# Hashed attention beside a gated feed-forward layer: a unit's maximum is spread three steps behind its own transposes

## The chip, the cores and the metric

The kernel runs on one core of a Trainium2 chip. The metric is the device time of one execution in microseconds; three executions of the kernel as it stood are given below, and one more was recorded by the hardware profiler. The engines are TensorE (PE in the rows, with its weight loads as PEld), VectorE (DVE), ScalarE (ACT), GpSimd (POOL) and SyncE (SP), which issues most transfers.

## The reference

```python
# attention: 2 batches, 8 heads, 768 positions, 64 columns a head
q_bucket = np.sum(((q @ proj) > 0) * 2 ** np.arange(6), axis=-1)   # k_bucket likewise
mask = q_bucket[:, :, :, None] == k_bucket[:, :, None, :]
scores = np.where(mask, scale * np.matmul(q, k.transpose(0, 1, 3, 2)), -1e9)
scores = scores - np.max(scores, axis=-1, keepdims=True)
attn = np.exp(scores); attn = attn / (attn.sum(-1, keepdims=True) + 1e-9)
x = np.matmul(attn, v)                       # then reshaped to 1536 x 512
# layer 1: w_gate, w_val 512 x 1536, w_out 1536 x 512
g = x @ w_gate
x = (g / (1 + np.exp(-g)) * (x @ w_val)) @ w_out
# layer 2: w_in 512 x 2048, w_out 2048 x 512
h = x @ w_in
out = (np.maximum(h, 0) + alpha * np.minimum(h, 0)) @ w_out
```

## The kernel before

**The attention** is cut into 24 items (a batch, a pair of heads, 256 queries), and each item into two units, one for each head: 48 units. A unit passes through four parts, each a Python generator whose yields are the steps that the rest of the kernel counts:

- `banks` (three steps): the scores S of 768 keys by 256 queries, two 128-key blocks to a PSUM bank (L283, L284, tag S, three banks); ACT copies each bank to the SBUF tile `se` (L285); DVE takes maxima over the blocks into `m2`, of which there is one buffer (L291, L293).
- `top` (one step, `s_mt`): PE transposes `m2` (tile `mt`, L303, and L309 in the second chunk, behind a DVE maximum on L307), and DVE reduces it to the maximum of each query, `mq` (L304 or L310).
- `back` (one step): `s_mb` transposes `mq` again, spread over all partitions (tile `mb`, L315); `s_sub` subtracts it from the scores on DVE (L320, 128 x 1536); `s_exp` takes the exponential on ACT (L325).
- `values` (three steps): six pairs of matmuls `po` with the values (L333), and behind the second head the denominators and the rounding of the result (L339 to L362).

The four parts of different units are woven together. A list gives each part a slot: that of the unit's number plus 0, 1, 2 and 3 (`LAGS`, L33). From slot 6 on a slot holds, in this order, the `banks` of unit s, the `top` of unit s-1, the `back` of unit s-2 and the `values` of unit s-3: eight steps. So a unit's `back` comes nine steps behind its `top`, and its `values` nine steps behind its `back`.

**The layers.** Tokens go through in three chunks of 512. The attention of chunk 0 (16 units) runs with the preparation of the first weights alone; the bank tag of `mt` and `mb` is then G, with two banks. From there on `stage1(0)` and `stage1(1)`, layer 1 of chunks 0 and 1, run with the attention of chunks 1 and 2 beside them: the main loop takes 1.9 attention steps for each yield of `stage1` (`RATES`). In this part of the program `mt` and `mb` both lie in the tag T (L812), and T has one bank (L779):

```python
    at.nb = dict(S=3, T=1, G=2, Y=1, po=1)
    at.tag = dict(m="T", hp="S", po=("po", "po"))
```

`stage1(2)` and the three `stage2` calls then run without attention. Layer matmuls are L642 to L644 (tiles `gp` and, in layer 2, `hp`) and L647 to L649 (`op`), each 128 x 512; the gates' work on DVE is L622 and L625, on ACT L619 and L634, on POOL L637. In `stage1(0)` each weight is read from memory for the first time as raw 64-bit words and converted: L539 on ACT, L540 and L542 on DVE, L544 on POOL, then split into two parts on ACT (L579) and on POOL or DVE in turn (L586).

The order of the work on each engine follows the order of these calls, except that the framework's scheduler lets an instruction whose inputs and buffers are free pass one that has to wait. Each engine executes its own list in order.

Of the kernel before, what the change touches and what calls it, by code (L numbers as in the profile page):

```python
# [32 lines left out]
LAGS = (0, 1, 2, 3)  # L33

OLDER = 6
# [13 lines left out]
def lsh_attention_moe_kernel(  # L49
# [19 lines left out]
    GQ = 256  # L69
    NG = S // GQ  # L70
    NPAIR = H // 2
# [4 lines left out]
    W = 512  # L76
# [74 lines left out]
    def load_v(it):  # L151

        t = at.sm.tile([P, NC, 3 * D], F32, tag="vv", name="vv", bufs=4)
        VV[it.b, it.p] = t
        nc.gpsimd.memset(t[:, :, D:2 * D], 1.0)
        for x in range(2):
            nc.sync.dma_start(out=t[:, :, 2 * x * D:(2 * x + 1) * D], in_=vP[it.b, 2 * it.p + x])

    def load_k(it):

        it.nat = wp.tile([P, S], F32, tag="raw64", name="nat", bufs=RAWB)
        nc.sync.dma_start(out=it.nat, in_=kview2(it))
        nc.gpsimd.dma_start(out=KA(it)[0:D], in_=kview(it))

    def load_q(it, eng=nc.sync):
        it.qr = at.sm.tile([P, 2, GQ], F32, tag="qr", name="qr", bufs=2)
        eng.dma_start(out=it.qr, in_=qview(it))
# [56 lines left out]
    def prep(it):  # L224

        def rest():
            pass

        todo = []
        if it.first:  # L230
            todo += [lambda x=x: rest_k(it, x, nc.gpsimd if POOL_K[x] else nc.vector) for x in range(2)]
            todo += [lambda x=x: copy_k(it, x) for x in range(2)]
        if it.first and it.b > 0:
            todo += [lambda: load_v(it)]
        todo += [lambda: round_q(it), lambda: rest_q(it)] + [rest] * (1 if it.first else 4)
        if it.first:
            todo += hash_k(it, 0) + hash_k(it, 1)
        todo += hash_q(it)
        last = todo[-1]

        def end():
            last()
            it.ready = True

        todo[-1] = end
        return todo

    def load(it):
        if it.first and it.b > 0:
            load_k(it)  # L250
        load_q(it)
# [7 lines left out]
    def first_item(it):  # L259
        ka, kb = KA(it), KB(it)  # L260
        for x in range(2):
            nc.scalar.activation(out=ka[0:D, x], in_=it.nat[x * D:(x + 1) * D, :], func=AF.Copy)
        round_q(it)
        for x in range(2):
            rest_k(it, x, nc.vector)
        nc.vector.tensor_tensor(out=it.QB[0:D], in0=it.qr[0:D], in1=f32(it.QA)[0:D], op=ALU.subtract)
        for x in range(2):
            nc.scalar.activation(out=kb[0:D, x], in_=it.nat[x * D:(x + 1) * D, :], func=AF.Copy)
        for fn in hash_q(it) + hash_k(it, 0, "G") + hash_k(it, 1, "G"):
            fn()  # L270
        it.ready = True

    def s_bank(u, j):
        it = u.it
        if j == 0:
            u.se = at.sm.tile([P, NC, GQ], F32, tag="se", name="se", bufs=at.nse)
        pt = at.ps.tile([P, 2, GQ], F32, tag="S", name="S", bufs=at.nb["S"])
        u.pt.append(pt)
        qa, qb = it.QA[:, u.x, :], it.QB[0:KR, u.x, :]
        ka, kb = KA(it)[:, u.x, :], KB(it)[0:KR, u.x, :]  # L280
        for i in range(2):
            sl = slice((2 * j + i) * P, (2 * j + i + 1) * P)
            nc.tensor.matmul(pt[:, i, :], lhsT=ka[:, sl], rhs=qa, start=True, stop=False)  # L283
            nc.tensor.matmul(pt[:, i, :], lhsT=kb[:, sl], rhs=qb, start=False, stop=True)  # L284
        nc.scalar.activation(out=u.se[:, 2 * j:2 * j + 2, :], in_=pt, func=AF.Copy)  # L285

    def s_max(u, j):

        if j == 1:
            u.m2 = at.sm.tile([P, 2, GQ], F32, tag="m2", name="m2", bufs=1)  # L290
            nc.vector.tensor_tensor(out=u.m2, in0=u.pt[1], in1=u.se[:, 0:2, :], op=ALU.max)  # L291
        else:
            nc.vector.scalar_tensor_tensor(out=u.m2, in0=u.pt[2], scalar=FLOOR, in1=u.m2, op0=ALU.max, op1=ALU.max)  # L293
            u.pt = None

    def s_mt(u):

        tp = at.ps.tile([P, 2, 2, P], F32, tag=at.tag["m"], name="mt", bufs=at.nb[at.tag["m"]])
        u.mq = at.sm.tile([P, 2, 1], F32, tag="mq", name="mq", bufs=2)
        if at.halves:  # L300
            for j in range(2):
                for h in range(2):
                    nc.tensor.transpose(tp[:, j, h, :], u.m2[:, h, j * P:(j + 1) * P], ident)  # L303
            nc.vector.tensor_reduce(out=u.mq, in_=tp.rearrange("p a b c -> p a (b c)"), axis=AX.X, op=ALU.max)  # L304
        else:
            m1 = u.m2[:, 0, :]
            nc.vector.tensor_tensor(out=m1, in0=m1, in1=u.m2[:, 1, :], op=ALU.max)  # L307
            for j in range(2):
                nc.tensor.transpose(tp[:, j, 0, :], m1[:, j * P:(j + 1) * P], ident)  # L309
            nc.vector.tensor_reduce(out=u.mq, in_=tp[:, :, 0, :], axis=AX.X, op=ALU.max)  # L310

    def s_mb(u):
        bc = at.ps.tile([P, 2, P], F32, tag=at.tag["m"], name="mb", bufs=at.nb[at.tag["m"]])
        for j in range(2):
            nc.tensor.transpose(bc[:, j, :], u.mq[:, j, :].to_broadcast([P, P]), ident)  # L315
        u.mx = bc.rearrange("p a b -> p (a b)")

    def s_sub(u):

        nc.vector.scalar_tensor_tensor(  # L320
            out=u.se, in0=u.se, scalar=FLOOR, in1=u.mx[:, None, :].to_broadcast([P, NC, GQ]),
            op0=ALU.max, op1=ALU.subtract)

    def s_exp(u):
        nc.scalar.activation(out=u.se, in_=u.se, func=AF.Exp, scale=SCALE)  # L325
# [31 lines left out]
    def s_xh(it):  # L357
        nc.scalar.activation(out=xcols(it)[0], in_=it.xf, func=AF.Copy)
# [7 lines left out]
    for b in range(B):  # L366
        order = [(p, g) for g in range(NG) for p in range(NPAIR)]
# [10 lines left out]
    def attention():  # L378

        us = []  # L380
        for it in items:
            for x in range(2):
                u = Bag()
                u.it, u.x, u.pt = it, x, []
                us.append(u)
        todo = []

        def queue(i):

            if i + 2 < len(items):  # L390
                todo.extend(prep(items[i + 2]))
            if i + 3 < len(items):
                n = 2 if items[i + 2].first and i > 0 else 1
                todo.insert(min(len(todo), n), lambda: load(items[i + 3]))

        def step():

            for _ in range(2 if at.alone else 1):
                if todo:
                    todo.pop(0)()  # L400

        load_k(items[1])
        load_q(items[1])
        load_v(items[0])
        first_item(items[0])
        for i in (2, 3):
            load_k(items[i])
            load_v(items[i - 1])
        load_q(items[2])
        load_v(items[3])  # L410
        todo.extend(prep(items[1]))

        def banks(u):
            for j in range(3):
                s_bank(u, j)
                if j == 2:
                    s_max(u, 1)
                step()
                yield
            s_max(u, 2)  # L420
            if u.x == 1:
                queue(u.it.i)

        def top(u):
            s_mt(u)
            step()
            yield

        def back(u):
            s_mb(u)  # L430
            s_sub(u)
            s_exp(u)
            step()
            yield

        def values(u):
            for j in range(3):
                s_pv(u, j)
                if j == 2 and u.x == 1:
                    s_den(u.it)  # L440
                    s_out(u.it)
                    s_xh(u.it)
                    s_xl(u.it)
                step()
                yield

        order = []
        for i, u in enumerate(us):
            for k, part in enumerate((banks, top, back, values)):
                slot = i + LAGS[k]  # L450
                order.append(((slot, i, k) if slot < OLDER else (slot, k, i), part, u))
        order.sort(key=lambda o: o[0])
        for _, part, u in order:
            if part is banks:
                while not u.it.ready:
                    todo.pop(0)()
            yield from part(u)
# [33 lines left out]
    late = [w for w in o2 if w not in early]  # L491
# [290 lines left out]
    first_load(items[0])  # L782
    setup()
    side = attention()

    def more():
# [17 lines left out]
    k = 0  # L804
# [103 lines left out]
```

## Time and profile before

| | |
|---|---|
| median of three executions | 874.92 us (872.17 to 876.06) |
| the profiled execution, its own time | 873.3 us |
| its span, first to last instruction | 871.5 us |
| PE busy | 824.7 us, 95% |
| DVE busy | 525.4 us, 60% |
| ACT busy | 448.4 us, 51% |
| POOL busy | 364.5 us, 42% |

The stretches of the span: attention of chunk 0 alone to about 128 us; layer 1 of chunk 0 with the attention of chunk 1 beside it to about 305 us and a little beyond; layer 1 of chunk 1 with the last attention to about 480 us; layer 1 of chunk 2 to about 605 us; layer 2 to the end. A busy share says how much of a stretch an engine had an instruction in work; matmuls overlap in the pipeline, so PE's idle time is read from what the rows print in brackets (the idle time before an instruction, and what ended it).

### The profile page before, as it was taken

What the parts mean: (1) busy time and instruction counts of PE and PEld (TensorE: products, weight loads), DVE (VectorE), ACT (ScalarE), POOL (GpSimd) and SP (SyncE); (2) the same over time, 40 slices, a digit from 0 to 9 for tenths busy, and PEclk for the clock granted to TensorE, in tenths of its full rate; (3) what the DMA queues carried; (4) which work ended last, traced back from release to release, by engine and by line L of the source; (5) the groups of instructions that cost most, each with busy time, mean ns of one, the idle gap of its engine ahead of it and who ended that gap; (6) DMA issues with size and microseconds to landing.
All of it is one profiled execution on the core that took longest, in us unless ns stands there. A gap on an engine that the chain in (4) does not pass through costs nothing.

```text
span 871.5 us, 11218 instructions
## 1 busy us (share of the span) xinstructions
PE 824.7 (95%) x4022; PEld 685.0 (79%) x4022; DVE 525.4 (60%) x789; ACT 448.4 (51%) x738; POOL 364.5 (42%) x304
## 2 busy tenths in 40 slices
PE   5989889899989999999999998989999999999997
PEld 3777777687777888888888786877888888888886
DVE  5877979888878856666665373645433343334332
ACT  6877977687766654655543233313333333334331
POOL 4211527675554533322322353623544354435441
PEclk9999999999999999999999999999999999999999
DMA  9120356786565437555445678886000300010001
GB/s 218 57 73 25 111 163 203 226 279 226 184 227 184 158 133 265 170 181 180 157 159 193 213 257 291 313 283 223 1 0 1 146 1 1 0 49 1 1 0 49
DMA packets 57287, 122.03 MB, mean 140 GB/s; under 512 B 16912, under 2 KB 29200, under 8 KB 56720
## 3 DMA queue, kind: packets, MB, share of 16 engines
q1 hardware_dynamic: 56080, 118.51, 39.9%
q0 software_dynamic: 1008, 2.75, 1.6%
q8 instruction: 32, 0.52, 0.2%
q14 instruction: 23, 0.19, 0.1%
q10 hardware_dynamic: 144, 0.05, 0.0%
HBM read 94.03 MB, written 27.26 MB: 139 GB/s over the span
## 4 chain that ended last, share of the span: by engine, by line
PE 62%; DVE 12%; DMA 10%; ACT 9%; issue 4%; POOL 2%; SPq 0%; ACTq 0%; DVEq 0%; POOLq 0%
PE po L333 8%; DMA raw<-in_wblk_dram 7%; PE gp L643 6%; PE gp L642 6%; PE gp L644 6%; PE op L648 5%; PE hp L643 5%; PE hp L644 5%; PE op L647 5%; PE op L649 5%; PE hp L642 5%; DMA wb<-w 2%; PE S L283 2%; PE S L284 2%; ACT se L285 2%
## 5 line engine op out<-in xcount | busy, mean ns | idle before, releaser
L637 POOL TENSOR_TENSOR gl<-ex,gh 128x512 fp32r<-128x512 f32 x84 | 110.2, 1311 | 183.5 <-ACT gh L634 183.3
L333 PE MATMUL po<-se,vv 128*128 128x256 f32 x576 | 143.6, 384 | 3.7 <-ACT se L325 3.7
L642 PE MATMUL gp<-xh,wb 128*128 128x512 f32 x288 | 121.2, 421 | 4.0 <-DMA wb<-w 3.9
L333 PEld LDWEIGHTS po<-se,vv 128*128 128x128 f32 x576 | 106.5, 191 | 20.4 <-ACT se L325 5.2
L628 DVE TENSOR_SCALAR ex<-hp,al 128x512 f32<-128x512 f32 x48 | 36.1, 751 | 135.7 <-PE hp L644 135.7
L644 PE MATMUL gp<-xh,wb 128*128 128x512 f32 x288 | 113.1, 393 | 0.0
L643 PE MATMUL gp<-xl,wb 128*128 128x512 f32 x288 | 112.9, 392 | 0.0
L634 ACT ACTIVATE gh<-ex 128x512 fp32r<-128x512 f32 x84 | 52.9, 630 | 107.1 <-DVE ex L631 67.8
L579 ACT ACTIVATE wb<-w 128x512 fp32r<-128x512 f32 x96 | 60.4, 631 | 92.1 <-PE hp L644 78.2
L544 POOL TENSOR_TENSOR wt<-wt,wr 128x512 int32<-128x512 int32 x48 | 63.5, 1327 | 87.3 <-DVE wt L542 44.7
L325 ACT ACTIVATE se<-se 128x1536 f32<-128x1536 f32 x48 | 71.3, 1485 | 49.7 <-DVE se L320 49.5
L285 ACT ACTIVATE se<-S 128x512 f32<-128x512 f32 x144 | 80.2, 592 | 22.9 <-PE S L284 19.1
L320 DVE SCALAR_TENSOR_TENSOR se<-se,mb 128x1536 f32<-128x1536 f32 x48 | 83.8, 1746 | 3.2 <-PE mb L315 3.1
L283 PE MATMUL S<-QA,kt 128*128 128x256 f32 x288 | 81.7, 310 | 2.8 <-ACT se L285 1.6
L284 PE MATMUL S<-qb,kt 76*128 76x256 f32 x288 | 75.4, 291 | 2.7 <-ACT qb L204 1.7
L642 PE MATMUL hp<-xh,wb 128*128 128x512 f32 x192 | 74.7, 389 | 0.0
L643 PE MATMUL hp<-xl,wb 128*128 128x512 f32 x192 | 74.7, 389 | 0.0
L644 PE MATMUL hp<-xh,wb 128*128 128x512 f32 x192 | 74.7, 389 | 0.0
L647 PE MATMUL op<-wb,gh 128*128 128x512 f32 x192 | 74.7, 389 | 0.0
L648 PE MATMUL op<-wb,gh 128*128 128x512 f32 x192 | 74.7, 389 | 0.0
L649 PE MATMUL op<-wb,gl 128*128 128x512 f32 x192 | 74.7, 389 | 0.0
L586 POOL TENSOR_TENSOR wb<-w,wb 128x512 fp32r<-128x512 f32 x48 | 62.3, 1297 | 23.7 <-ACT wb L579 23.7
(98 smaller groups left out, 1667.8 us busy)
## 6 DMA issues: line engine op xcount, KB each, us to landing
wb<-w SPq DMA_DIRECT2D x72, 512.0 KB, 4.0
raw<-in_wblk_dram SPq DMA_DIRECT2D x68, 512.0 KB, 4.3
w<-wb SPq DMA_DIRECT2D x36, 512.0 KB, 3.1
qr<-in_q_dram SPq DMA_DIRECT2D x24, 256.0 KB, 3.0
nat<-in_k_dram SPq DMA_DIRECT2D x8, 384.0 KB, 3.6
vv<-in_v_dram SPq DMA_DIRECT2D x16, 192.0 KB, 5.2
whole<-wt SPq DMA_DIRECT2D x12, 256.0 KB, 2.1
w<-whole SPq DMA_DIRECT2D x12, 256.0 KB, 6.3
```

The costliest lines, as they stand in the source:

```text
L283: nc.tensor.matmul(pt[:, i, :], lhsT=ka[:, sl], rhs=qa, start=True, stop=False)
L284: nc.tensor.matmul(pt[:, i, :], lhsT=kb[:, sl], rhs=qb, start=False, stop=True)
L285: nc.scalar.activation(out=u.se[:, 2 * j:2 * j + 2, :], in_=pt, func=AF.Copy)
L320: nc.vector.scalar_tensor_tensor(out=u.se, in0=u.se, scalar=FLOOR, in1=u.mx[:, None, :].to_broadcast([P, NC, GQ]), op0=ALU.max, op1=ALU.su ...
L333: nc.tensor.matmul(it.po[:, u.x, :], lhsT=VV[it.b, it.p][:, kb, u.x * D:u.x * D + P], rhs=u.se[:, kb, :], start=kb == 0, stop=kb == NC - 1)
L637: nc.gpsimd.tensor_tensor(out=l, in0=ex, in1=f32(h), op=ALU.subtract)
L642: nc.tensor.matmul(pt, lhsT=h, rhs=ah, start=first, stop=False)
L643: nc.tensor.matmul(pt, lhsT=h, rhs=al_, start=False, stop=False)
L644: nc.tensor.matmul(pt, lhsT=l, rhs=ah, start=False, stop=last)
L647: nc.tensor.matmul(pt, lhsT=gh, rhs=h, start=first, stop=False)
L648: nc.tensor.matmul(pt, lhsT=gh, rhs=l, start=False, stop=False)
L649: nc.tensor.matmul(pt, lhsT=gl, rhs=h, start=False, stop=last)
```

## The change

From unit 14 on (2 x 4 x 2 - 2), `back` gets the slot of the unit's number plus 1, and stands last in it. A slot from 16 on then holds the `banks` of unit s, the `top` of unit s-1, the `values` of unit s-3 and the `back` of unit s-1. A unit's `back` comes four steps behind its own `top`, with the three steps of an older unit's `values` in between, and its `values` come thirteen steps behind its `back`. Nothing is added or removed.

```diff
         order = []
         for i, u in enumerate(us):
+            beside = i >= 2 * NPAIR * (W // GQ) - 2
             for k, part in enumerate((banks, top, back, values)):
-                slot = i + LAGS[k]
-                order.append(((slot, i, k) if slot < OLDER else (slot, k, i), part, u))
+                slot = i + (1 if part is back and beside else LAGS[k])
+                late = 4 if part is back and beside else k
+                order.append(((slot, i, k) if slot < OLDER else (slot, late, i), part, u))
         order.sort(key=lambda o: o[0])
```

In the changed program every line below these has a number higher by two: L642 becomes L644, L540 becomes L542, L542 becomes L544, L586 becomes L588.

**PE, one unit beside layer 1 of chunk 0** (the transposes that the trace of before has at 170.11 us). Here `mt` and `mb` are the two users of the bank T, `gp` is layer 1, `hp` the hashes, `po` the values. Before:

```order
L303 MATMUL mt<-ident,m_1572 128x128 x4
L642 MATMUL gp<-xh,wb 128x512
L643 MATMUL gp<-xl,wb 128x512
L644 MATMUL gp<-xh,wb 128x512
L642 MATMUL gp<-xh,wb 128x512
L643 MATMUL gp<-xl,wb 128x512
L644 MATMUL gp<-xh,wb 128x512
L192 MATMUL hp<-kt_124,skh 44x384
L315 MATMUL mb<-ident,mq 128x128 x2
L193 MATMUL hp<-kt_124,skl 44x384
```

Of the change, the same unit; the first piece left out is three more `hp` and six `gp`, the second the rest of six `gp`:

```order
L303 MATMUL mt<-ident,m_1577 128x128 x4
L333 MATMUL po<-se,vv 128x256 x2
L192 MATMUL hp<-kt_124,skh 44x384
...
L333 MATMUL po<-se,vv 128x256 x4
L644 MATMUL gp<-xh,wb 128x512
...
L315 MATMUL mb<-ident,mq 128x128 x2
L192 MATMUL hp<-kt_124,skh 44x384
```

Between the four `mt` and the two `mb` stood six `gp` and one `hp`; now there are twelve `gp`, six `po` and four `hp`. From `mb` to the next four `mt` there were eighteen `gp`, twelve `S`, six `po` and ten `hp`; now there are twelve `gp`, twelve `S` and eight `hp`, four of them of 256 columns.

**DVE, the same unit.** Before, from the first maximum of the next unit to the subtraction L320:

```order
L291 TENSOR_TENSOR m_1572<-S,se 128x512
L304 TENSOR_REDUCE mq<-mt 128x2
L293 SCALAR_TENSOR_TENSOR m_1572<-S,m_1572 128x512
L625 SCALAR_TENSOR_TENSOR ex<-ex,gp 128x512
L320 SCALAR_TENSOR_TENSOR se<-se,mb 128x1536
L542 SCALAR_TENSOR_TENSOR wt<-raw_1620,wt 128x512
L586 TENSOR_TENSOR wb<-wt,wb 128x512
```

Of the change:

```order
L291 TENSOR_TENSOR m_1577<-S,se 128x512
L304 TENSOR_REDUCE mq<-mt 128x2
L293 SCALAR_TENSOR_TENSOR m_1577<-S,m_1577 128x512
L588 TENSOR_TENSOR wb<-wt,wb 128x512
L542 TENSOR_SCALAR wt<-raw_1669 128x512
L542 TENSOR_SCALAR wt<-raw_1732 128x512
L544 SCALAR_TENSOR_TENSOR wt<-raw_1669,wt 128x512
L544 SCALAR_TENSOR_TENSOR wt<-raw_1732,wt 128x512
L320 SCALAR_TENSOR_TENSOR se<-se,mb 128x1536
```

Two instructions stood between the reduction L304 and the subtraction L320; now six do, the weight work that used to follow.

**ACT, at the end of chunk 0's attention** (`wr` is the conversion of a raw weight, L325 the exponentials). Before:

```order
L285 ACTIVATE se<-S 128x512 x3
L539 ACTIVATE wr<-raw_1009 128x512
L325 ACTIVATE se<-se 128x1536
L204 ACTIVATE qb_67<-mk 12x256 x2
L325 ACTIVATE se<-se 128x1536
L339 ACTIVATE den<-po 64x256 x2
```

Of the change:

```order
L285 ACTIVATE se<-S 128x512 x3
L541 ACTIVATE wr<-raw_1009 128x512
L325 ACTIVATE se<-se 128x1536 x2
L204 ACTIVATE qb_67<-mk 12x256 x2
L339 ACTIVATE den<-po 64x256 x2
```

The first exponential stands behind the same raw weight in both; the second passed two short copies.

## Rows read from the trace of the kernel before

**Rows 1.** The page: span, and busy time of each engine.
```profile
span 871.5 us, 11218 instructions
PE 824.7 (95%) x4022; PEld 685.0 (79%) x4022; DVE 525.4 (60%) x789; ACT 448.4 (51%) x738; POOL 364.5 (42%) x304
```

**Rows 2.** Stretches: start:end, length, then PE, PEld, DVE, ACT, POOL busy; clock.
```profile
128.00:305.00 177.00, 165.41 (x868) 138.17 (x867) 150.84 (x222) 126.85 (x215) 101.91 (x84) 1.00 0.64 211
305.00:480.00 175.00, 174.17 (x897) 147.25 (x896) 110.53 (x177) 90.92 (x147) 50.17 (x43) 1.00 0.51 179
```

**Rows 3.** What PE waited for from 128 to 305 us: total, times, longest.
```profile
PE mb L315 <- DVE mq L304: 9.8, 10, 2.1
```

**Rows 4.** The same from 305 to 480 us.
```profile
PE mb L315 <- DVE mq L310: 0.8, 2, 0.6
```

**Rows 5.** PE in order of time: start, length, count, idle before.
```profile
169.63 0.28 PE L283 MATMUL S<-QA,kt 128*128 128x256 f32 x1
169.74 0.28 PE L284 MATMUL S<-qb,kt 76*128 76x256 f32 x1
...
170.11 0.60 PE L303 MATMUL mt<-ident,m 128*128 128x128 f32 x4
...
171.24 0.40 PE L642 MATMUL gp<-xh,wb 128*128 128x512 f32 x1
171.48 0.39 PE L643 MATMUL gp<-xl,wb 128*128 128x512 f32 x1
...
171.94 0.33 PE L192 MATMUL hp<-kt,skh 128*44 128x384 f32 x1
173.74 0.40 PE L315 MATMUL mb<-ident,mq 128*128 128x128 f32 x2 [1.47 <-DVE mq L304]
```

**Rows 6.** DVE in order of time, the same place.
```profile
172.31 0.69 DVE L291 TENSOR_TENSOR m<-S,se 128x512 f32<-128x512 f32 x1
172.91 0.68 DVE L304 TENSOR_REDUCE mq<-mt 128x2 f32<-128x512 f32 x1
173.51 0.68 DVE L293 SCALAR_TENSOR_TENSOR m<-S,m 128x512 f32<-128x512 f32 x1
...
174.71 1.75 DVE L320 SCALAR_TENSOR_TENSOR se<-se,mb 128x1536 f32<-128x1536 f32 x1
```

**Rows 7.** The longest wait for the reduction: PE, then DVE.
```profile
157.51 0.60 PE L303 MATMUL mt<-ident,m 128*128 128x128 f32 x4
162.13 0.40 PE L315 MATMUL mb<-ident,mq 128*128 128x128 f32 x2 [2.07 <-DVE mq L304]
161.31 0.67 DVE L304 TENSOR_REDUCE mq<-mt 128x2 f32<-128x512 f32 x1
```

**Rows 8.** What DVE waited for from 128 to 305 us.
```profile
DVE wt L540 <- DMA raw<-in_wblk_dram: 5.7, 3, 4.4
DVE wt L540 <- POOL wb L586: 5.2, 5, 2.2
DVE xf L349 <- ACT den L339: 4.8, 5, 1.4
DVE ex L622 <- ACT ex L619: 2.9, 3, 2.1
```

**Rows 9.** DVE's reductions and weight conversions there: shortest, median, longest in ns.
```profile
L304 DVE TENSOR_REDUCE mq<-mt x15: 669/676/681, 128.1 to 295.7; 128x2 f32<-128x512 f32 x15
L540 DVE TENSOR_SCALAR wt<-raw x31: 378/428/1858, 131.3 to 299.7; 128x512 int32<-128x512 int32 x31
L542 DVE SCALAR_TENSOR_TENSOR wt<-raw,wt x31: 676/693/1696, 131.7 to 300.1; 128x512 int32<-128x512 int32 x31
```

**Rows 10.** The end of chunk 0's attention: PE, two of ACT, and a stretch.
```profile
116.07 4.39 PE L333 MATMUL po<-se,vv 128*128 128x256 f32 x12 [2.25 <-ACT se L325]
113.98 0.66 ACT L539 ACTIVATE wr<-raw 128x512 int32<-128x512 uint32 x1 [1.46 <-DMA raw<-in_wblk_dram]
116.00:119.00 3.00, 2.93 (x7) 2.40 (x8) 1.80 (x4) 2.33 (x4) 0.00 (x0) 0.50 0.44 175
```

## The prediction

> **What bounds the kernel now.** The page first: PE is busy for 824.7 of 871.5 us, no other engine for more than 60% [rows 1]. So what shortens PE's list, or takes idle time out of it, can shorten the kernel; the change takes no instruction away, so only idle time is to be had. Next the stretches where attention stands beside layer 1. From 128 to 305 us PE is busy for 165.4 of 177 us, DVE for 150.8; from 305 to 480 us PE for 174.2 of 175 [rows 2]. The list of PE's waits says which wait ends last in the first stretch: 9.8 of the 11.6 us that PE is idle are `mb` (L315) waiting for the reduction L304 on DVE, ten times, the longest 2.1 us [rows 2, 3], while fifteen units are reduced there [rows 9]. In the second stretch it is 0.8 us [rows 4].
>
> Why `mb` waits there is not in the row, since the `mq` that it reads was reduced a whole unit earlier. It comes from the bank: `mt` and `mb` share the single bank T, so the `mb` of unit s-2 stands behind the `mt` of unit s-1 and must wait until DVE has reduced that one. The rows show it at 170 us: four `mt` from 170.11, six `gp` and one `hp` on PE, and then 1.47 us of nothing until `mb` at 173.74; on DVE the reduction started only at 172.91, behind the maximum L291, and ended at 173.59 [rows 5, 6]. DVE is late, and PE had only 2 us of other work.
>
> **The change, part by part.**
>
> *The wait of `mb`.* Paces, start to start: `gp` 0.23 (171.48 less 171.24), S 0.11 to 0.12, four `mt` about 0.4 (0.60 less the last one's tail) [rows 5]. The others I estimate by these: a `po`, which is 256 columns in a slower form, at 0.22, near a `gp`; `hp` of 384 columns as 1.5 S, 0.18; two `mb` as half of four `mt`, 0.2. Before, `mb` stood six `gp` and one `hp` behind the first `mt`: 0.4 + 1.4 + 0.2 = 2.0 us. Now twelve `gp`, six `po` and four `hp` lie between: 0.4 + 2.8 + 1.3 + 0.7 = 5.2; units without `hp` there have 4.5. The reduction ended 3.5 us behind the first `mt` at this place (173.59 less 170.11), and 4.5 at the place of the longest wait (161.98 less 157.51) [rows 5 to 7]. So if DVE is no later than it is now, every one of these waits is covered by other work: 9.8 + 0.8 = 10.6 us, the most that the change can give in this way [rows 3, 4].
>
> *The wait that can take its place.* The next `mt` needs the bank T back, so it now waits for the subtraction L320 behind the same unit's `mb`. From `mb` to the next `mt` PE had over 8 us of other work (eighteen `gp`, twelve S, six `po`, ten `hp`); now twelve `gp`, twelve S and eight `hp`: 0.2 + 2.8 + 1.4 + 1.2 = 5.6 here, 4.4 without hashes. On DVE the subtraction stands further down: between L304 and it stood L293 and L625, and now stand L293, a weight remainder, and two conversions of two instructions each. At 0.6 start to start for an operation of 512 columns from PSUM, 0.69 for L542 and 0.43 for L540 that is 0.6 + 0.7 + 2 x 0.43 + 2 x 0.69 = 3.5 us, then 1.75 for L320 itself [rows 6, 9]. With reductions that end 3.5 to 4.5 behind the first `mt`, the subtraction ends 8.8 to 9.8 behind it; PE's list from `mt` to `mt` is 5.2 + 5.6 = 10.8 with hashes and 4.5 + 4.4 = 8.9 without. So a late unit without hashes can lose up to 0.9 us, the others nothing. The bounds are nothing (all as early as at 170 us) and 0.9 x 15 = 13.5 us (all as late as at 157 us, none with hashes). I take 2 us, near the lower one, since five of fifteen units had no wait at all and only the longest wait goes with 4.5.
>
> *What is queued behind.* A later L320 means a later L325 on ACT, and behind it the copies of the next scores. The `values` of a unit now come thirteen steps behind its `back`, before nine, so the later exponential costs them nothing; if that cover were gone, each would cost PE what L320 is late, 1 to 2 us. The score copies have three S banks to run ahead. SP and POOL issue the same transfers in the same number; `back` issues none.
>
> *The end of chunk 0's attention.* Here the new order begins, still with the two G banks. PE's one large wait is 2.25 us for an exponential that stood on ACT behind a raw weight's landing, and the next 3 us ran at a granted clock of 0.50, the lower level of 1.2 GHz [rows 10]. ACT has the same conversion ahead of the same exponential in both orders, so I leave this at nothing; if the pause and its slow stretch went away, 2.25 us and half of the 3 would come back, some 4, and as much is lost if they double.
>
> *The sum.* 10.6 - 2.0 = 8.6 us: 873.3 us, the profiled execution's own time, less 8.6 is 864.7. That execution lies 1.6 below the median of the three, so for the median 866.3. Nothing later takes it back: from 305 to 480 us PE has hardly an idle microsecond in which it could go [rows 2], and what follows runs without attention.
>
> **The rivals.**
>
> *DVE sets the pace.* In the first stretch DVE is busy for 150.8 us, and 18.6 us of its idle time are waits for others than PE (5.7 + 5.2 + 4.8 + 2.9) [rows 2, 8]. If all of these stay, the stretch can't be shorter than 169.4, a gain of 7.6, so the forecast stands just at that bound. Its conversions also stretch: L540 has a median of 428 ns and a longest of 1858, L542 693 and 1696 [rows 9]. One more such case in each unit, at the 1.0 us between L542's median and longest, is 15 us of DVE time; with half of the 18.6 absorbed that makes 150.8 + 15 + 9.3 = 175.1, a gain of 1.9 and with the second stretch 2.7: 872.2 for the median; half as many cases give about 869. For it speaks that DVE is late at all; against it that nothing in the order brings DVE more work, only less idle time. The Trainium skill, SBUF — State Buffer, section "Who interferes with whom", says that a DVE instruction in a two-port mode or with two SBUF inputs and a GpSimd instruction hold one shared pair of ports as a lock, so that whichever starts second waits in full. By that rule the same POOL work in less time makes more long conversions, and the time would be that of this rival. The long cases fit it, but no row here shows who held what.
>
> *Slower: the bank T is waited for on the other side.* If DVE is as late at every unit as at 157.51 us and one conversion between L304 and L320 takes the long 1.7 us, the subtraction ends 10.8 behind the first `mt`, against 8.9 to 10.8 of PE's work, some 9.8 in the mean: 1.0 x 15 = 15 us of new waits against 10.6 taken away, 879.3 for the median. It decides from 0.7 us a unit (10.6 / 15). Against it: while PE stands at `mt`, DVE catches up, and DVE's work fits into the stretch with 26 us to spare [rows 2].
>
> *No change.* The waits of `mb` end, but DVE's lateness is met at the next thing that PE needs from it (a gate bank, a hash, an S bank), and the stretch keeps its 177 us: 874.9 for the median. For it: DVE's share of the stretch is 85% already. Against it: all waits of PE but those for `mb` are under 2 us together (11.6 less 9.8) [rows 2, 3].
>
> **How the numbers follow.** The forecast has 0.57, DVE's pace 0.22, no change 0.11, slower 0.10. Half a per cent is 4.4 us, about what a measurement of this kernel can tell from no change. The forecast and half of the second case lie beyond it, faster: 0.68. The other half, no change and 0.04 of the slower case, whose price stands just at the line, are within: 0.26. Slower: 0.06. The range goes from 860.5 (all of the 10.6 and 4 from the end of chunk 0's attention, off 874.9) to 875.5 (no change), and leaves out the slower case and a little below.
>
> **What would show it.** In the profile after: the wait of `mb` for L304 from 128 to 305 us under 2 us; a new wait of `mt` for L320 of 0 to 4 us; PE busy for over 96% of that stretch and DVE for about 89%; the stretch some 8 us shorter, the later ones as they were. I am wrong if `mt` waits as long as `mb` did, if reductions end more than 4.5 us behind their `mt`, if PE's waits for gates or hashes grow, or if the pause at 116 us changes by more than 1 us.

## The result, and the profile after

The change made the kernel slower: 884.18 us (882.48 to 885.63, four runs) against 874.32 for the kernel before on the same chip, a ratio of 1.0108, 95% interval 1.0083 to 1.0134. The forecast was 866.3, with a range that ended at 875.5.

| | before | after |
|---|---|---|
| span of the profiled execution | 871.5 us | 880.9 us |
| first layer matmul of chunk 0 | 129.3 us | 128.8 us |
| first matmul with the last (36th) weight of `stage1(0)` | 327.2 us | 337.3 us |
| from there to the last layer 1 matmul | 278.4 us | 278.0 us |

All of the difference arises beside layer 1 of chunk 0. The stretches of the changed kernel (columns as in [rows 2]):

```profile
128.00:305.00 177.00, 161.18 (x817) 134.61 (x816) 147.20 (x207) 118.08 (x201) 98.55 (x79) 0.96 0.64 206
305.00:480.00 175.00, 174.31 (x907) 149.46 (x906) 118.06 (x186) 94.21 (x157) 52.84 (x45) 1.00 0.50 178
```

PE got through 817 matmuls in the first stretch, before 868 [rows 2], and its clock, full before, is 0.96 on the mean. DVE is busy for less than before in this window, but gets through less there, 207 instructions for 222. Over the whole of `stage1(0)` DVE is busy for 170.3 us where it was 162.6, though no work was added: some of its instructions take longer, as the bullet on DVE's conversions shows. What PE waited for in the changed kernel from 128 to 314 us (total, times, longest):

```profile
PE po L333 <- DVE xf L355: 3.5, 1, 3.5
PE hp L192 <- DVE mk L198: 3.5, 2, 2.1
PE S L283 <- DVE mk L198: 2.2, 1, 2.2
PE mt L303 <- DVE se L320: 2.1, 2, 1.5
PE S L284 <- ACT qb L204: 1.9, 2, 1.0
PE hp L192 <- ACT se L285: 1.8, 1, 1.8
PE gp L644 <- ACT xh L358: 0.5, 1, 0.5
PE S L283 <- ACT se L285: 0.2, 1, 0.2
```

No row of `mb` is left, where [rows 3] had ten waits and 9.8 us. In its place stand waits for everything else that DVE and ACT make: hash bits (L198), the output chain (L355), copies of scores (L285). Together they make 15.7 us, some 4 more than before, in fewer and longer pauses: the longest was 2.1, now it is 3.5.

The place of the longest pause, DVE of the changed kernel in order of time:

```profile
153.22 0.67 DVE L304 TENSOR_REDUCE mq<-mt 128x2 f32<-128x512 f32 x1
153.82 0.67 DVE L293 SCALAR_TENSOR_TENSOR m<-S,m 128x512 f32<-128x512 f32 x1
154.42 0.67 DVE L627 SCALAR_TENSOR_TENSOR ex<-ex,gp 128x512 f32<-128x512 f32 x1
155.01 0.68 DVE L588 TENSOR_TENSOR wb<-wt,wb 128x512 fp32r<-128x512 f32 x1
155.62 0.41 DVE L542 TENSOR_SCALAR wt<-raw 128x512 int32<-128x512 int32 x1
156.06 0.69 DVE L544 SCALAR_TENSOR_TENSOR wt<-raw,wt 128x512 int32<-128x512 int32 x1
156.75 1.45 DVE L542 TENSOR_SCALAR wt<-raw 128x512 int32<-128x512 int32 x1
158.23 1.66 DVE L544 SCALAR_TENSOR_TENSOR wt<-raw,wt 128x512 int32<-128x512 int32 x1
159.82 1.74 DVE L320 SCALAR_TENSOR_TENSOR se<-se,mb 128x1536 f32<-128x1536 f32 x1
161.48 0.43 DVE L349 STREAM_TRANSPOSE xf<-den 128x256 f32<-128x256 f32 x1
...
162.63 1.67 DVE L173 TENSOR_TENSOR kt<-nat,kt 64x768 fp32r<-64x768 f32 x1
164.33 0.45 DVE L351 STREAM_TRANSPOSE den<-r 128x256 f32<-128x256 f32 x1
164.81 0.86 DVE L355 TENSOR_TENSOR xf<-po,den 64x256 f32<-64x256 f32 x2
```

and PE there:

```profile
154.09 0.38 PE L315 MATMUL mb<-ident,mq 128*128 128x128 f32 x2
...
161.61 0.66 PE L303 MATMUL mt<-ident,m 128*128 128x128 f32 x4 [1.55 <-DVE se L320]
165.81 0.77 PE L333 MATMUL po<-se,vv 128*128 128x256 f32 x1 [3.54 <-DVE xf L355]
```

The maximum was spread at 154.09, but the subtraction ended at 161.56, behind two conversions that took 4.2 us. Before, two instructions (L293 and L625) stood between L304 and L320. Behind the late L320 now stands the output chain L349 to L355, with a key operation (the remainder of rounded keys, L173, 1.67 us) in the middle of it, and `po` has one bank: the next `po` waits for it. So the forecast's one new wait (`mt` for L320, 1.55 us here) is there, and it is not the largest.

Conversions are not all that stands ahead. Before the wait of 2.15 us for hash bits that ended at 191.37 us, DVE had one conversion instruction of 0.69 us, but a key operation of 2.48 us, and then the output chain and L320:

```profile
183.38 2.48 DVE L173 TENSOR_TENSOR kt<-nat,kt 64x768 fp32r<-64x768 f32 x1
...
187.59 1.72 DVE L320 SCALAR_TENSOR_TENSOR se<-se,mb 128x1536 f32<-128x1536 f32 x1
...
190.71 0.60 DVE L198 TENSOR_SCALAR mk<-hp,ck 44x384 f32<-44x384 f32 x1
```

Another part of the loss is in the clock. Stretches of the changed kernel round this place and round two other pauses (the last three columns are the granted clock, DMA share and GB/s):

```profile
160.80:164.20 3.40, 0.66 (x4) 0.42 (x4) 3.37 (x5) 2.61 (x4) 2.89 (x3) 1.00 0.72 217
164.20:171.00 6.80, 5.19 (x12) 4.20 (x13) 6.69 (x11) 5.63 (x10) 4.73 (x4) 0.50 0.83 217
171.00:190.00 19.00, 18.22 (x98) 15.13 (x96) 16.78 (x22) 10.66 (x18) 13.21 (x11) 1.00 0.64 218
191.50:194.90 3.40, 3.40 (x13) 2.85 (x13) 2.70 (x5) 3.26 (x8) 1.61 (x2) 0.50 1.07 245
256.30:259.70 3.40, 3.40 (x14) 3.19 (x15) 0.96 (x2) 3.33 (x7) 1.27 (x1) 0.51 0.04 17
```

PE did four matmuls in the 3.4 us to 164.2, and then ran for 6.8 us at a granted clock of 0.50, the lower level of 1.2 GHz. The other two follow pauses of 2.15 us and of 2.21 and 0.96 us (the waits for L198, and one for `qb`). The profile of before has no such stretch between 128 and 340 us, though it has a pause of 2.1.

To put sizes on this, the time of `stage1(0)` (first layer matmul to the first with the last weight) is split for each kernel. Each matmul has a pace, the time from its start to the next one's (`gp` 0.229 us, S 0.119, and so on). What a step takes over its pace by more than 0.3 us is counted as waiting, what matmuls started in stretches of half clock take over it as clock. The rest, the work at full pace with small gaps, came to 184 to 186 us in every kernel of this study, so the split closes:

| stage 1 of chunk 0 | length | waits | clock | us at half clock |
|---|---|---|---|---|
| before | 197.9 | 13.6 | 0.0 | 0.0 |
| after | 208.5 | 19.6 | 4.1 | 13.7 |
| new order beside chunk 0 only | 210.5 | 21.4 | 4.9 | 17.1 |
| new order beside chunk 1 only | 199.0 | 13.0 | 1.6 | 3.4 |
| older unit, same place | 214.0 | 21.6 | 7.4 | 23.9 |
| conversions held back | 212.5 | 23.6 | 3.1 | 10.2 |
| moved one step only | 206.1 | 16.4 | 5.6 | 13.7 |
| after, remainders on POOL | 207.2 | 18.1 | 5.1 | 13.7 |
| before, remainders on POOL | 206.9 | 17.4 | 4.2 | 10.2 |
| before, half the conversions' DVE work | 196.8 | 10.7 | 2.0 | 6.8 |
| after, the same | 200.1 | 13.1 | 2.4 | 6.8 |
| before, none of it | 200.3 | 13.8 | 1.0 | 3.4 |
| after, the same | 196.0 | 9.4 | 2.6 | 6.8 |

Of the 10.6 us between the first two rows, 6.0 are longer waits and 4.1 are matmuls at half clock. (These waits are larger than those of the profile's list, which counts only time in which no matmul was in the pipeline. A step close to the limit of 0.3 us can move half a microsecond from one column to another.)

Each row is one execution, and that of the kernel before is the shortest of its order. Four more traces have the old order in this stage: the new order beside chunk 1 only, and three kernels below that add pauses later on. Their stages took 199.0 to 202.0 us, with 13 to 16 us of waits and 1.6 to 2.2 us of clock. Against the mean of all five, 200.2 us, the two traces of the new order (208.5 and 210.5) are 9.3 us longer: some 6 us are waits and some 3 are clock.

### The profile page after: what moved, and what is told of

Same layout as the page of the kernel before. It is cut to its first block, busy times and chain, and to the rows that moved or that the text cites. A ratio compares the mean times of both kernels' runs of the same rounds, so it can differ in the third digit from the quotient of the medians.

```text
span 880.9 us, 11193 instructions
## 1 busy us (share of the span) xinstructions
PE 831.6 (94%) x4022; PEld 693.5 (79%) x4022; DVE 533.9 (61%) x789; ACT 446.9 (51%) x738; POOL 366.3 (42%) x304
## 4 chain that ended last, share of the span: by engine, by line
PE 65%; DVE 10%; ACT 9%; DMA 8%; issue 4%; POOL 3%; SPq 0%; POOLq 0%; ACTq 0%; DVEq 0%
PE po L333 8%; PE gp L644 7%; PE gp L645 7%; PE gp L646 7%; DMA raw<-in_wblk_dram 6%; PE op L649 5%; PE hp L645 5%; PE hp L644 5%; PE op L650 5%; PE op L651 5%; PE hp L646 5%; ACT se L285 2%; PE S L284 2%; PE S L283 2%; DVE se L320 2%
## 5 line engine op out<-in xcount | busy, mean ns | idle before, releaser
L333 PEld LDWEIGHTS po<-se,vv 128*128 128x128 f32 x576 | 108.8, 194 | 24.1 <-ACT se L325 4.5
L644 PE MATMUL gp<-xh,wb 128*128 128x512 f32 x288 | 122.9, 427 | 4.3 <-DMA wb<-w 2.3
L646 PE MATMUL gp<-xh,wb 128*128 128x512 f32 x288 | 114.5, 398 | 0.0
L320 DVE SCALAR_TENSOR_TENSOR se<-se,mb 128x1536 f32<-128x1536 f32 x48 | 83.7, 1744 | 20.1 <-PE mb L315 19.9
L285 ACT ACTIVATE se<-S 128x512 f32<-128x512 f32 x144 | 79.5, 590 | 30.1 <-PE S L284 23.8
L325 ACT ACTIVATE se<-se 128x1536 f32<-128x1536 f32 x48 | 71.2, 1485 | 30.1 <-DVE se L320 29.9
L644 PE MATMUL hp<-xh,wb 128*128 128x512 f32 x192 | 74.7, 389 | 0.0
L588 POOL TENSOR_TENSOR wb<-w,wb 128x512 fp32r<-128x512 f32 x48 | 62.6, 1303 | 23.3 <-ACT wb L581 23.3
```

Source lines behind the costliest of these rows:

```text
L320: nc.vector.scalar_tensor_tensor(out=u.se, in0=u.se, scalar=FLOOR, in1=u.mx[:, None, :].to_broadcast([P, NC, GQ]), op0=ALU.max, op1=ALU.su ...
L333: nc.tensor.matmul(it.po[:, u.x, :], lhsT=VV[it.b, it.p][:, kb, u.x * D:u.x * D + P], rhs=u.se[:, kb, :], start=kb == 0, stop=kb == NC - 1)
L644: nc.tensor.matmul(pt, lhsT=h, rhs=ah, start=first, stop=False)
L646: nc.tensor.matmul(pt, lhsT=l, rhs=ah, start=False, stop=last)
```

## The experiments

Theory A: in the new order the subtraction L320 stands on DVE behind weight conversions, and hash bits, output chain and score copies stand behind it; DVE's lateness is met in fewer but longer pauses. Theory B: a good part of the loss is the lower clock after these pauses. Rivals: the single bank T or PE's own order (C), and the short way from a unit's own transposes to its spread maximum.

**Where the loss is.** The first two kernels have the new order for some units only. The first:

```diff
-            beside = i >= 2 * NPAIR * (W // GQ) - 2
+            beside = 14 <= i < 30
```

> The new order for units 14 to 29 only (beside layer 1 of chunk 0); from unit 30 on the order of before. Theory A (in the new order the subtraction L320 stands on DVE behind weight conversions, and the hash bits, the output chain and ACT's score copies stand behind it; its lateness is met in fewer and longer pauses of PE): all of the loss is here, some 884 us, 9 to 10 over before, with the pauses of up to 3.5 us and the stretches of half clock of the change. Theory C (the single bank T itself, in any stretch): half of the loss, some 879.

Measured: 886.69 us, ratio to before 1.0145 (1.0113 to 1.0178). As theory A expected, all of the loss is in these units. The second:

```diff
-            beside = i >= 2 * NPAIR * (W // GQ) - 2
+            beside = i >= 30
```

> The new order from unit 30 on only (beside layer 1 of chunk 1, where no weight is converted); ahead of it the order of before. Theory A: 873 to 875 us, no change, the waits of mb at 0.8 us or less and no new pause over 1 us. Theory C (the bank T or PE's own order makes new waits): 876 to 880.

Measured: 874.21 us, ratio 0.9987 (0.9961 to 1.0012). The same order on PE, with the same bank T, costs nothing where no weight is converted; it also gives nothing, since [rows 4] had but 0.8 us to give. That speaks for A, against C.

**Whose maximum is spread.** The back of the older unit at the new place:

```diff
-                slot = i + (1 if part is back and beside else LAGS[k])
+                slot = i + LAGS[k]
                 late = 4 if part is back and beside else k
```

> The back of the older unit (two behind, as before the change), but moved to the end of the slot, behind the values as in the change: the same turn of the bank T on PE, the subtraction in the same place on DVE, and mb reads a maximum that is a unit old. Theory A (the place of the subtraction on DVE decides, not whose maximum is spread): within 3 us of the change, 881 to 887. Rival (the short distance between a unit's own top and back decides): near the kernel before, 872 to 877.

Measured: 885.77 us, ratio 1.0138 (1.0090 to 1.0186). The maximum is a unit old and the loss is no smaller. What counts is the place in the slot, not whose maximum it is. The loss is not made up alike in every part: in this kernel a unit's `values` come four steps behind its `back`, and from 128 to 320 us `po` waits for exponentials for 3.3 us, a wait that the change does not have.

**Conversions held back.** In the change, conversions that fall due between a unit's top and its subtraction are queued behind the subtraction, with their parts on ACT and POOL:

```diff
+            ws.hold = not at.alone and u.it.i < 16
...
+            ws.hold = False
+            with tc.issue_after(u.sub.ins):
+                flush()
...
-            round64(raw.pop(i), wt[i].bitcast(I32))
+            held.append(lambda: round64(raw.pop(i), wt[i].bitcast(I32)))
```

> The change, with the DVE conversions of raw weights that fall due between a unit's top and its subtraction L320 held and issued behind that subtraction. Nothing is added or removed. Theory A: the pauses for hash bits, output chain and score copies shrink below 2 us and the time comes to that of before or under it, 866 to 876. Theory C (bank T): the waits and the time of the change remain, 880 to 885.

Measured: 886.55 us, ratio 1.0147 (1.0115 to 1.0179): theory A's expectation failed, and the time is above the range of theory C too. What DVE waited for from 128 to 315 us in this kernel, and what PE waited for:

```profile
DVE se L320 <- PE mb L315: 16.8, 6, 7.3
```

```profile
PE gp L661 <- POOL wb L603: 8.3, 6, 2.8
PE gp L659 <- ACT wb L596: 3.8, 4, 1.7
PE hp L192 <- DVE mk L198: 1.9, 1, 1.9
```

The wait for the output chain went, and that for hash bits fell from 5.7 us to 2.2, as A has it. But DVE then stood idle at L320 for 16.8 us, waiting for `mb` on PE, and the weights came late instead (12.1 us of `gp` waiting for POOL and ACT). Neither of the two places that were tried for the conversions is good: ahead of L320 they make it late, behind it they leave DVE idle and come late themselves.

**Moved by one step only.** Before, with the back of the older unit behind the first of the three steps of values:

```diff
...
+                late = 3.5 if part is back and i >= 16 else k
+                if part is values and i >= 16:
+                    order.append(((slot, 3, i), first, u))
+                    order.append(((slot, 4, i), rest, u))
...
```

> The kernel before, with the back of the older unit (two behind) moved by one step only, behind the first of the three steps of values, from unit 16 on: some two po and more gp between mt and mb, the subtraction three to five DVE rows behind the reduction where the change has four to fourteen. Theory A: part of the 9.8 us of mb's waits goes without the pauses of the change, 866 to 873. Theory C: any move of mb toward the next mt costs, 876 to 882.

Measured: 879.23 us, ratio 1.0060 (1.0037 to 1.0082). Theory A's expectation failed, and the time lies in the range of theory C (any move of `mb` toward the next `mt` costs). C's own wait is not in the trace, though: no `mt` waits for L320. `mb` still waited for 8.9 us, `po` for 1.9 us for an exponential, and 5.6 us went to the clock. A third of the way brings about half of the loss.

**DVE lighter.** Without the second DVE operation of each conversion in `stage1(0)`, in both kernels:

```diff
-        nc.vector.scalar_tensor_tensor(out=a, in0=t[:, :, 1], scalar=-0x40000000, in1=a,
+        if not getattr(ws, "busy", False):
+            nc.vector.scalar_tensor_tensor(out=a, in0=t[:, :, 1], scalar=-0x40000000, in1=a,
...
```

> The kernel before, without the second DVE operation of each weight conversion beside layer 1 of chunk 0 (24.5 us of DVE's 155.7 in that stretch; the converted weights are then not those of the reference). Theory A (DVE's lateness is what PE meets): the waits of mb for the reduction go below 4 us, and the time falls by 5 to 10 us, to 865 to 870. Theory C (the turn of the bank T): waits as before, 872 to 875.

Measured: 868.33 us, ratio 0.9933 (0.9911 to 0.9955). The time is in theory A's range, but the waits of `mb` fell only to 6.8 us where under 4 were expected.

> The change, without the same DVE operation. Theory A: with DVE lighter by some 25 us the pauses over 1 us and the half-clock stretches between 128 and 315 us go, and the time is no longer above that of the kernel before with the same cut: 864 to 871. Theory C (the turn of the bank T itself, or PE's order): 7 us or more above that kernel, 875 to 882.

Measured: 873.38 us, ratio 0.9992 (0.9965 to 1.0020). The change is still behind, by 5.0 us where it was 9.9, with the longest wait for hash bits at 2.4. Neither theory had that. (That wait is the one behind the key operation of 2.48 us.) Open was whether the rest is the other half of the conversions, or the order of the attention's own work on DVE. So both DVE operations were left out; POOL's addition then reads the raw word itself:

```diff
+        if getattr(ws, "busy", False):
+            pin(nc.gpsimd.tensor_tensor(out=a, in0=t[:, :, 1], in1=r, op=ALU.add))
+            return
```

> The kernel before, without both DVE operations of each weight conversion beside layer 1 of chunk 0 (some 45 us of DVE's 155.7 in that stretch; POOL's addition reads the raw word itself, so the weights are not those of the reference). Theory A: the waits of mb for the reduction fall below 3 us, 864 to 868.

Measured: 875.55 us, ratio 0.9999 (0.9977 to 1.0020).

> The change, without the same two DVE operations. Theory A (all of the loss is DVE's lateness behind conversions): no longer than the kernel before with the same cut, within 2 us of it or under it, and no pause over 1.5 us from 128 to 315 us. Rival (the order itself sets the subtraction against hash bits and output chain on DVE, conversions or not): 3 us or more above it, with the waits for hash bits (L198) and the output chain (L355) still there.

Measured: 872.26 us, ratio 0.9956 (0.9935 to 0.9976). Now the new order is the faster one, by 3.3 us on the same chip. What PE waited for in the last kernel from 128 to 325 us:

```profile
PE S L283 <- ACT se L285: 3.8, 1, 3.8
PE S L284 <- ACT qb L204: 1.9, 1, 1.9
PE hp L192 <- DVE mk L198: 1.0, 1, 1.0
```

and in its partner, the old order without conversions on DVE:

```profile
PE mb L315 <- DVE mq L304: 10.3, 6, 3.2
```

Without conversions between L304 and L320 the waits for hash bits shrink to 1.0 us and that for the output chain goes; the old order keeps its `mb` waits. (This trace is of the fastest of twelve executions, 867.87 us, so its waits are on the low side.) The sign of the change hangs on the conversions: +9.9 us with all of them, +5.0 with half, -3.3 with none.

But the two orders do not move alike. Against the whole kernel before on the same chip, the new order goes from 9.9 us above it to 1.2 below with half of the conversions' work and 4.5 below with none. The old one goes to 6.2 below and then back to 1.2 below. So of the turn in the last step 3.3 us are the new order's gain and 5.0 the old one's loss. Why the old order loses there is open. ACT waits longer for raw weights in both kernels without conversions (25.4 and 26.6 us from 128 to 320 us, 14.1 in the kernel before), and the expectation for the old order was wrong: with DVE some 44 us lighter `mb` waits no less. The reduction is late there although DVE has little to do, since DVE itself stands waiting ahead of it: before the longest wait 8.3 us for ACT's copies, behind a transfer of keys, before others for gates or weight parts. The 3.8 us of the new order are of the same kind, with ACT waiting for a raw weight.

**Remainders on POOL.** All weight remainders of layer 1 on POOL, in both orders:

```diff
-            n, m = PL
+            n, m = (1, 1) if i < NW1 else PL
```

> The change, with all the weight remainders of layer 1 on POOL, where every second one is on DVE: 16 operations of DVE less beside layer 1 of chunk 0, POOL's more. Theory A: DVE is lighter by some 14 us and the pauses for hash bits and output chain shrink, 872 to 880. Rival (POOL's longer turn makes weights late, and DVE's conversions longer): 882 to 892, with gp waiting for weights.

Measured: 880.71 us, ratio 1.0079 (1.0049 to 1.0108).

> The kernel before, with all the weight remainders of layer 1 on POOL. If DVE's lateness is what PE meets there, the waits of mb shrink by half or more and the time falls to 868 to 872; if POOL's longer turn makes DVE wait as much as it saves, 873 to 877.

Measured: 881.92 us, ratio 1.0061 (1.0038 to 1.0084). Both expectations for the old order missed, and the new order came out just above theory A's range. This takes work from DVE without making it earlier: in the new order DVE now waits for POOL before its conversions, the row of its waits from 128 to 320 us being

```profile
DVE wt L542 <- POOL wb L588: 26.6, 20, 3.5
```

where the change has 8.9 us in ten waits. In the old order the same wait went from 5.2 us [rows 8] to 20.0. The new order can't be told from the change as it was (the intervals overlap); the old one lost some 5 us.

**The pauses by themselves.** To separate a pause from what it does to the clock, pauses were put into layer 1 of chunk 2 of the kernel before, where no attention runs: one transpose on PE, a chain of n + 1 copies on ACT, a second transpose behind it, and all later layer matmuls queued behind that.

```diff
...
+        with tc.issue_after(ws.last.ins):
+            nc.tensor.transpose(z[:, :P], ident, ident)
+        nc.scalar.activation(out=y.rearrange("p (a b) -> p a b", b=P), in_=z[:, None, :P].to_broadcast([P, 3, P]), func=AF.Copy)
+        for _ in range(n):
+            nc.scalar.activation(out=y, in_=y, func=AF.Copy)
+        return nc.tensor.transpose(z[:, P:2 * P], y[:, :P], ident)
...
```

> The kernel before, with four pauses put into layer 1 of chunk 2, where no attention runs: PE makes a transpose, ACT a chain of eight small copies behind it, PE a second transpose behind the chain, and all later layer matmuls stand behind that; some 4 us each, 16 in all. Theory B (after a long pause PE runs at half clock for 3.4 us or more): four stretches of 3.4 to 6.8 us at a clock of 0.5 behind the pauses, the time longer than before by the sum of the pauses and 5 to 12 us more, 895 to 903. Rival (the pauses alone cost): by their sum and no more, some 890.

> The same with eight pauses of half the chain, some 2 us each, 16 in all. Theory B: as in the trace, where pauses of 2 us were followed by half clock in some places and not in others, two to six stretches of 3.4 us, 3 to 10 us beyond the sum of the pauses. Rival: the sum of the pauses, some 890.

> The same with twenty pauses of one copy each, some 0.8 to 1 us, 16 to 20 in all. Theory B: no more half clock than in the kernel before; the time longer by the sum of the pauses, 891 to 895, and not beyond it by more than 2 us. Rival (half clock comes from the sum of the idle time and not from long pauses): as far beyond the sum as the four long ones.

Measured: 901.14, 907.11 and 894.49 us; ratios 1.0267 (1.0232 to 1.0303), 1.0320 (1.0272 to 1.0368) and 1.0194 (1.0158 to 1.0230). The stage in the profile of each, split as above (a pause is the time from the last `gp` ahead of it to the first behind it, less 0.228):

| layer 1 of chunk 2 | length | pauses put in | clock | other waits | rest |
|---|---|---|---|---|---|
| before | 106.4 | 0 | 0.0 | 7.4 | 99.0 |
| four long | 130.8 | 23.6 (4.8 to 6.4 idle each) | 7.0 | 1.4 | 98.8 |
| eight of half the chain | 138.1 | 27.0 (2.6 to 4.4 idle each) | 11.6 | 0.7 | 98.8 |
| twenty short | 125.7 | 24.9 (one of 2.1, the others under 1.1 idle) | 0.0 | 0.8 | 100.0 |

PE's stretches from 478 to 640 us, long, half, short (as in [rows 2]):

```profile
478.00:640.00 162.00, 138.21 (x575) 111.65 (x574) 71.66 (x98) 58.60 (x104) 60.35 (x46) 0.94 0.63 216
```

```profile
478.00:640.00 162.00, 136.97 (x551) 109.45 (x550) 68.32 (x91) 55.36 (x100) 57.22 (x44) 0.92 0.63 215
```

```profile
478.00:640.00 162.00, 143.45 (x630) 112.88 (x629) 78.67 (x102) 53.49 (x98) 63.97 (x49) 1.00 0.64 219
```

and PE behind the first long pause:

```profile
515.20 0.27 PE L691 MATMUL z<-ident 128*128 128x128 f32 x1
521.42 0.48 PE L695 MATMUL z<-ident,pz 128*128 128x128 f32 x1 [5.95 <-ACT pz L694]
...
522.55 0.63 PE L645 MATMUL gp<-xh,wb 128*128 128x512 f32 x1
522.98 0.63 PE L643 MATMUL gp<-xh,wb 128*128 128x512 f32 x1
...
524.90 0.40 PE L645 MATMUL gp<-xh,wb 128*128 128x512 f32 x1
525.13 0.39 PE L643 MATMUL gp<-xh,wb 128*128 128x512 f32 x1
```

The same matmul goes at 0.43 us until 524.6 and at 0.23 after. The short pauses together are as long as the long ones and cost nothing beyond their own length. Eight pauses of 2.6 us and more cost 11.6 us on top of 27.0, more than was expected; seven of them have a stretch of half clock, the one that began at 564.5 us has none. The chains came out longer than meant (23.6 and 27.0 us in place of 16), so the times alone don't tell the theories apart; the split does, in favour of B.

## Why the prediction was wrong

- **The wait of `mb`**, 10.6 us to be had: right. From 128 to 314 us no wait of `mb` is left.
- **The wait that can take its place**, `mt` for L320, 2 us: right in size, 2.1 us there and 0.7 in the next stretch, but partly by luck. The working had the subtraction end 8.8 to 9.8 us behind the first `mt`; it ended 8.7 to 14.3 behind it, 11.7 on the mean of fourteen units, where before it was 5.9. At five of them the reduction ended more than 4.5 us behind `mt`, one of the named signs of being wrong, and the larger of the two waits was 1.55 us where a late unit could lose 0.9. The sum stayed small while PE, held up elsewhere, came late to the bank as well. The slower rival put its price here, and had the wrong place: the bank T is not where the time went.
- **What is queued behind**: this is the step that failed. It said that a later L320 costs the values nothing, which held but for the output chain, and that "the score copies have three S banks to run ahead", so that the rest costs nothing. But the hashes `hp` lie in the same three banks, and their bits L198 and the output chain L355 are work of the same DVE, behind the same L320. The waits for the output chain, for hash bits, for ACT's copies of them (`qb`) and for score copies are 3.5 + 5.7 + 1.9 + 2.0 = 13.1 us by the profile's list, where before all waits but `mb` came to 1.8 (11.6 less 9.8) [rows 2, 3]. The term was some 11 us too low. The working looked at what waits for L320 by its data, and not at all that stands behind it on DVE by order. Growing waits for hashes were among its signs of being wrong, and they came.
- **The clock**: the prediction costed it at 116 us alone. In `stage1(0)` it cost 4.1 us in this trace, 2.6 more than on the mean of five traces of the old order, and the list of waits doesn't show it. Waits were summed whatever their lengths, ten of about 1 us like four of 1.8 to 3.5, and these are not equal.
- **DVE's conversions**: from 128 to 305 us their mean lengths rose from 657 to 797 ns (L542, before L540) and from 797 to 835 (L544, before L542), 0.18 us a conversion, and the four key operations L173 from 1534 to 1896. The rival on DVE's pace named this, and said that no row shows who held what. POOL's rows do. All thirteen long conversions of before, and 17 of the 18 of the changed kernel, began while a tensor operation of POOL was in work, and ended behind its end, the second instruction of a conversion by 0.55 us, the first by 0.28 to 0.32 (in before up to 0.64). Of the 49 short ones of before none began so; of the 41 of the changed kernel three did, at its very start or in its last 0.2 us. The rule of the Trainium skill on shared ports (SBUF — State Buffer, "Who interferes with whom"), that whichever of the two starts second waits in full, agrees with these rows. At the longest pause these two operations of POOL were in work, to 157.91 and 159.34 us, when the conversions of 156.75 and 158.23 us began:

```profile
156.20 1.71 POOL L639 TENSOR_TENSOR gl<-ex,gh 128x512 fp32r<-128x512 f32 x1 [2.46 <-ACT gh L636]
157.87 1.47 POOL L546 TENSOR_TENSOR wt<-wt,wr 128x512 int32<-128x512 int32 x1
```

  Four conversion instructions that take 2.2 us at their short lengths took 4.2 there, and L173 took 1.67 where its shortest is 0.95. So waiting for POOL is a good part of what makes L320 and the output chain late. The rival that named it still forecast a gain. How much time it costs by itself no run shows.
- **No change**: this rival named the right places ("a gate bank, a hash, an S bank"), but priced them at what was taken away. The lateness isn't handed on at its old size: gathered into fewer, longer pauses it grew by 6.0 us, and the clock added its part. PE was busy for 91% of the first stretch and DVE for 83%, where the prediction named 96 and 89.
- **The end of chunk 0's attention**: the pause there went from 2.25 to 1.70 us. The stretch of half clock near it was 6.8 us, from 106 us on, where it had been 3.4 from 116 on. Layer 1 starts 0.5 us earlier, so nothing of the loss is there.

What is shown: the loss is beside layer 1 of chunk 0 alone; it does not hang on whose maximum is spread; it halves with half of the conversions' DVE work and turns into a gain without it, though the old order's own loss has the larger part in that last step; and of the pauses put in, eleven of the twelve from 2.6 to 6.4 us met half clock, and none of the nineteen under 1.1 us and the one of 2.1. What stays open: no kernel moved the subtraction alone, with PE's order as it was, so the share of each follower of L320 (hash bits, output chain, exponential) is read from the trace and not from a run, and the same holds for the share of the waiting for POOL. None of the kernels that compute everything beat the one before; the nearest, the new order beside chunk 1 only, can't be told from it.

## What to carry to other kernels

When an instruction is moved, list all that stands behind it on its own engine, by order and not only by data, and ask for each who waits for it; here a wait that was taken off one place came back at the next. Weigh PE's pauses by their length: ten of 1 us cost 10, while one of 2 us or more may cost several more microseconds at half clock. To find whether an order is bad in itself, run both orders with the other work on that engine left out, and look at each against its own start: here the sign turned, and both orders had moved. When an instruction's length varies, lay its rows beside those of the other engines before calling it noise.

## What the runs showed of the hardware

- A `gp` of 512 columns goes at 0.229 us at full clock and 0.428 at a granted clock of 0.50. Beside the layers, stretches of half clock came as 3.4 or 6.8 us and often began before the pause had ended, as at 164.2 us, ahead of the `po` at 165.81.
- The length of a pause does not settle what follows it. From 120 to 640 us of all sixteen traces each pause of PE over 2.9 us met half clock or was followed by it. Of those from 1.6 to 2.9 us some did (one of 1.63 us in the kernel moved by one step) and some did not (2.07 us at 160 us and 2.90 at 524 us in the profile of before).
- The first half of the kernels with long, half and short pauses is the kernel before. In each a pause of 2.2 us that ended at 174 to 176 us, close behind another of 0.7 to 2.2, met 6.8 us of half clock; their `stage1(0)` took 201.4, 201.6 and 202.0 us against 197.9. That may be part of why executions of the kernel before lie between 870 and 881 us in this study.
- A weight conversion on DVE that began while a tensor operation of POOL was in work waited for its end: 0.38 to 0.43 us became up to 1.86 (L540), 0.69 up to 1.70 (L542).
- 16 operations taken off DVE and given to POOL made the old order 5 us slower, although POOL was busy for 58% of the first stretch [rows 2].
